# Second group's first layer interleaved with the end of the first group's second layer, and VectorE's order fixed by hand in that stage

## The chip, the cores and the metric

The kernel runs on one core of one Trainium2 chip. The metric is the device time in microseconds of one execution. A core has TensorE (matmuls; the profile calls it PE, and its weight loads PEld), VectorE (DVE), ScalarE (ACT), GpSimd (POOL) and SyncE (SP). Each of them works through its own list of instructions in order, and they wait for one another by semaphores. SyncE here only issues DMAs, and GpSimd issues those that fetch the weights.

## What is computed

```python
# q, k, v, a_re, a_im: (B=4, H=8, S=768, D=48)
mag = sqrt(a_re**2 + a_im**2)
a = (a_re + 1j * a_im) * minimum(mag, 0.999) / (mag + 1e-6)
for t in range(S):                       # a recurrence over complex states
    S_ = a[t][:, None] * S_ + outer(k[t], v[t])
    y[t] = q[t] @ S_.real
x = y as (B*S = 3072, H*D = 384)         # rows are tokens
h = x @ w_in                             # (3072, 2048)
out = (h * cos(h)) @ w_out               # (3072, 384)
```

The first part is an attention with gated, complex decay; the second is a two-layer block. The layer weights arrive as 64-bit floats, which the kernel turns into 32-bit floats itself.

## The kernel before, in words

**Tiling.** The 3072 tokens are cut into chunks of 128 steps, and two chunks make a group; there are twelve groups (`NG`). Within a chunk the recurrence is done with matmuls: the decays are turned to logarithms and angles, summed along the chunk by a matmul with a triangular matrix, and give factors for keys and queries.

**What a group does.** In order of the data:

- `g_log` takes logarithms of the decays on ScalarE and VectorE. `p_powers` sums them on TensorE (tile `lgs`) and takes exponentials. `g_angle` is an arctangent, `p_even` (three VectorE operations, which also store the last row to DRAM and read it back as `end`), `g_carry` (a carry from the chunk before, and a split in an upper half `hi` by ScalarE and a lower half `lo` by VectorE), `g_phase` (summed angles on TensorE, tile `phs`, a cast on ScalarE, a subtraction on VectorE).
- `p_apply`, `g_trig` and `g_stack` make the stacked keys `ks` and queries `qs`. From group 2 on `f_transpose` transposes them in blocks on VectorE (tile `tr`), and a round trip through DRAM (`moved`) gives `kT` and `qT`. Of these DMAs qT's comes last.
- For each chunk `f_scores` makes the scores on TensorE (tile `sc`) and masks them on VectorE (`atm`), `f_state` carries the state (`sp`), `f_out` makes the chunk's output (`yp`), which ScalarE copies to `yT`. `f_xt` stores yT to DRAM (`x`) and reads it back as `xT`, the input of the first layer.
- First layer: `mm1_sums` makes six matmuls into one tile `hp` (128 x 512), for two of the sixteen blocks of h; I call this a pair. `mm1_gate` follows: ScalarE takes the sine of it (with half pi added) and a square sum (`junk`), and VectorE multiplies (`gate`). A group has eight pairs.
- Second layer: `mm2` multiplies four (or `nj`) blocks of gates with w_out into the tile `op`, for one chunk. Only groups 0 and 1 do it in this plain form; later ones (`seventh`) use seven products of half size.

**PSUM.** There are eight banks of 128 x 512 floats: the pool `pa` has five (tag "a": lgs, phs, sc, sp, yp), and `pm` has three (tags "m", two, and "acc", one: hp, op, sum).

**Weights.** GpSimd's queue fetches w_in and w_out in 64-bit parts (`raw`), and `as_floats` converts each part: two VectorE operations, one on ScalarE, and a last one on VectorE. `convert(back[4:])` are the last four of w_out's eight parts, each two of the sixteen blocks j.

**Order.** TensorE's list is a chain in the order in which the program emits its matmuls, ScalarE's table functions are another, and `weave` spreads several lists of steps over a stage by fractions. For VectorE and the rest of ScalarE and SyncE a scheduler picks the order, except while `Ordered.by_hand` is true, when VectorE's and ScalarE's operations are chained as emitted; that holds for the start of group 0. The stage that changes is this one: group 0's second layer, the preparation of group 2, and group 1's first layer, one after another on TensorE. After it a loop over n from 2 on weaves the attention of group n, the second layer of n − 1, the preparation of n + 1 and the first layer of n. Inputs of a group beyond it (`load`) go through SyncE's queue, which also carries the DMAs of `f_xt`, `p_even`, `f_transpose` and the stores of the output.

Of the kernel before, what the change touches and what calls it, by code (L numbers as in the profile page):

```python
# [11 lines left out]
F32 = mybir.dt.float32  # L12
# [475 lines left out]
def fast_path(ctx, tc, q, k, v, a_re, a_im, moe_w_in, moe_w_out, out, least, odd, wide):  # L488
# [8 lines left out]
    DM, DF = moe_w_in.shape  # L497
    C = 128
    NCH = S // C
    G = 2  # L500
# [20 lines left out]
    pa = ctx.enter_context(tc.tile_pool(name="pa", bufs=5, space=PSUM))  # L521
# [22 lines left out]
    Y = [dict() for _ in range(N)]  # L544
# [104 lines left out]
    tail = {}  # L649
# [15 lines left out]
    class Ordered:  # L665


        by_hand, mark = False, {}

        def __init__(self, engine, name):  # L670
            self.engine, self.name = engine, name
# [1 line left out]
        def __getattr__(self, op):  # L673
            def call(**kw):
                ins = getattr(self.engine, op)(**kw)  # L675
                if Ordered.by_hand:
                    chain(ins, self.name)
                elif self.name in Ordered.mark:
                    behind(ins, Ordered.mark[self.name])
                return ins  # L680
            return call
# [120 lines left out]
    def p_even(g, i, n):  # L802


        x = X[g]
        u = cut(x["mag"], i, n)
        P, Q = cut(x["P"], i, n), cut(x["Q"], i, n)
        ins = [vector.scalar_tensor_tensor(out=u, in0=Q, scalar=HUGE, in1=P,
                                           op0=ALU.min, op1=ALU.mult)]
        for t in P, Q:  # L810
            ins.append(vector.scalar_tensor_tensor(out=t, in0=u, scalar=3.0, in1=t,
                                                   op0=ALU.subtract, op1=ALU.mult))

        for one_, what in zip(ins, ("carried", "split")):
            if what in x:
                behind(one_, x[what])
        row = x["row"][ds(i * DM, n * DM)]
        nc.sync.dma_start(out=row, in_=P[C - 1:C].rearrange("o x -> (o x)"))
        end = x["end"][:, ds(i * H, n * H)]
        for a in range(2):  # L820
            nc.sync.dma_start(out=end[ds(a * D, D)], in_=row.rearrange("(x d) -> d x", d=D))
# [8 lines left out]
    def p_apply(g, i, n):  # L830
        x = X[g]
        P, Q, u = (cut(x[name], i, n) for name in ("P", "Q", "mag"))
        vector.tensor_tensor(out=Q, in0=cut(x["k"], i, n), in1=Q, op=ALU.mult)
        vector.tensor_tensor(out=u, in0=cut(x["q"], i, n), in1=P, op=ALU.mult)

    def g_angle(g, i, n):

        at = cut(X[g]["tan"], i, n)
        special(out=at, in_=at, func=AF.Arctan)
# [4 lines left out]
    def g_carry(g):  # L844

        n, some = g * G, ds(C - 32, 32)
        if g >= PEG and n % NCH:
            head = cut(X[g]["tan"], 0, 1)[some]
            X[g]["carried"] = vector.scalar_tensor_tensor(
                out=head, in0=before(n)[some], scalar=carry[some], in1=head,  # L850
                op0=ALU.mult, op1=ALU.add)
        if g >= PEG:
            X[g]["split"] = upper_half(g, cut(X[g]["tan"], 0, G), 1.0 / math.pi)()
# [161 lines left out]
    def mm1_sums(g, jp):  # L1015
        x = X[g]
        x.setdefault("gate", {})
        order = x.setdefault("order", [])
        home = "mmc"[len(order) % 3]
        order.append(jp)  # L1020
        pool, tag, bufs = {"m": (pm, "m", 2), "c": (pm, "acc", 1)}[home]
        ps = pool.tile([C, 2, G * C], F32, tag=tag, name="hp", bufs=bufs)
        for ji in range(2):
            for dc in range(ND):
                matmul(ps[:, ji], lhsT=w_in[:, jp, dc, ts(ji, C)],
                       rhs=x["xT"][:, dc].rearrange("p g t -> p (g t)"),
                       start=(dc == 0), stop=(dc == ND - 1))
        x.setdefault("hp", {})[jp] = ps
# [16 lines left out]

    def mm2(g, i, j0, nj):
        if j0 == 0:
            Y[g * G + i]["op"] = pm.tile([C, DM], F32, tag="acc" if i == 0 else "m", name="op",
                                         bufs=1 if i == 0 else 2)
        ps = Y[g * G + i]["op"]  # L1050
        for j in range(j0, j0 + nj):
            matmul(ps, lhsT=X[g]["gate"][j // 2][:, j % 2, ts(i, C)], rhs=w_out[:, j],
                   start=(j == 0), stop=(j == NJ - 1))
        if j0 + nj == NJ:
            ot = msb.tile([C, DM], F32, tag="ot", name="ot")
            scalar.mul(out=ot, in_=ps, mul=1.0 / (in_scale * out_scale))
            nc.sync.dma_start(out=out[ts(g * G + i, C), :], in_=ot)
# [85 lines left out]
    def products(g, lo, hi):  # L1143
        if g < PLAIN:
            return []
        return [lambda p=p, part=part: seventh(g, p, part)
                for p in range(lo, hi) for part in range(2)]
# [4 lines left out]
    def weave(*parts):  # L1152

        items = []
        for p, (part, lo, hi) in enumerate(parts):
            part = list(part)
            items += [(lo + (hi - lo) * (i + 0.5) / len(part), p, t)
                      for i, t in enumerate(part)]
        for _, _, t in sorted(items, key=lambda x: x[:2]):
            t()  # L1160

    def each(step, g):
        return [lambda i=i, n=n: step(g, i, n) for i, n in spans(g)] if 0 <= g < NG else []

    def keys(g):

        if not 0 <= g < NG:
            return
        for i, n in spans(g):
            yield lambda i=i, n=n: g_trig(g, i, n)  # L1170
            yield lambda i=i, n=n: (g_stack(g, i, n), p_end(g, i, n))
            for name in "kT", "qT":
                if g >= PEG:
                    yield lambda i=i, n=n, name=name: f_transpose(g, i, n, name)
# [4 lines left out]
    def powers(g):  # L1179
        return [lambda i=i: p_powers(g, i) for i in range(G)]  # L1180

    def prods(g):
        if not 0 <= g < NG:
            return
        if g not in (1, 2):
            yield from powers(g)
            yield lambda: g_angle(g, 0, G)
        yield lambda: g_carry(g)
        yield lambda: (p_even(g, 0, G), p_apply(g, 0, G))

    def logs(g):
        yield from each(g_log, g)
        if 0 <= g and g + 1 < NG:
            yield lambda: load(g + 1, ("re", "im"))

    def phases(g):
        return [lambda i=i: g_phase(g, i) for i in range(G)] if 0 <= g < NG else []
# [11 lines left out]
    def first(g):  # L1209
        order = range(NJ // 2) if g < PLAIN else (0, 4, 1, 5, 2, 6, 3, 7)  # L1210
        return [lambda jp=jp: mm1(g, jp) for jp in order]

    def second(g, i):
        return [lambda j0=j0: mm2(g, i, j0, 4) for j0 in range(0, NJ, 4)] if g < PLAIN else []

    def convert(parts):
        return [lambda dst=dst, src=src: weight(dst, src)() for dst, src in parts]
# [22 lines left out]
    chain(nc.gpsimd.tensor_copy(out=alls, in_=one_b.to_broadcast([C, C])), "gpsimd")  # L1240
    early = [weight(dst, src) for dst, src in into[:RAW]]
    chain(nc.gpsimd.tensor_copy(out=exact, in_=ones), "gpsimd")
    Ordered.by_hand = True
    preload("natural_log_exp_and_others")
    busy(27)
    one, two = (log_steps(0, i, 1) for i in range(2))
# [16 lines left out]
    g_stack(0, 0, 1)  # L1263
    p_apply(0, 1, 1)
    g_stack(0, 1, 1)
    Ordered.by_hand, Ordered.mark = False, dict(tail)
    steps = log_steps(1, 0, G)
    log = [lambda: next(steps, None)]
    for t in (turned(0, 0, "kT") + turned(0, 0, "qT") + early[:1]
# [8 lines left out]
    def sums(g, lo, hi):  # L1278
        return [lambda jp=jp: mm1_sums(g, jp) for jp in range(lo, hi)]

    def gates(g, lo, hi):
        return [lambda jp=jp: mm1_gate(g, jp) for jp in range(lo, hi)]

    later = convert(into[RAW:])
    for t in (sums(0, 0, 2) + [lambda: g_angle(1, 0, G)] + later[:1] + phases(1)[:1]
# [5 lines left out]
          (keys(1), 0.3, 0.8), (convert(back[:1]), 0.9, 1.0))  # L1291
    over = [t for i in range(G) for name in ("kT", "qT") for t in turned(1, i, name)]
    weave((over, 0.0, 0.2), (chunks(1), 0.2, 1.0), (convert(back[1:4]), 0.1, 1.0),
          (logs(2), 0.7, 0.71))
    both = [t for pair in zip(second(0, 0), second(0, 1)) for t in pair]
    weave((both, 0.0, 0.5), (convert(back[4:]), 0.0, 0.3), (powers(2), 0.3, 0.34),
          ([lambda: g_angle(2, 0, G)], 0.35, 0.36), (prods(2), 0.36, 0.4),
          (phases(2), 0.47, 0.53), (keys(2), 0.53, 0.6), (first(1), 0.5, 1.0))
    room.close()
    stage.update(pool=ctx.enter_context(tc.tile_pool(name="late", bufs=1)), bufs=1)  # L1300
    for n in range(2, NG):
        weave((mixes(n - 1, 2, 4), 0.0, 0.12), (logs(n + 1), 0.0, 0.02), (chunks(n), 0.0, 0.36),
              (second(n - 1, 0), -0.08, 0.28), (products(n - 1, 0, 3), 0.0, 0.36),
              (prods(n + 1), 0.25, 0.27), (second(n - 1, 1), 0.4, 0.56),
              (products(n - 1, 3, 7), 0.4, 0.56), (phases(n + 1), 0.44, 0.54),
              (keys(n + 1), 0.53, 0.66), (quarters() if n == PLAIN else [], 0.4, 0.9),
              (last_quarter() if n == PLAIN else [], 0.9, 1.0), (first(n), 0.56, 1.0),
              (mixes(n, 0, 2), 0.9, 1.0), (guarded(n - 1, per) if n > 3 else [], 0.1, 0.9))
# [77 lines left out]
```

## Time and profile before

| | |
|---|---|
| median of 3 runs | 670.77 us (670.17 to 672.28) |
| profiled execution | 672.38 us; its span 670.6 us |
| TensorE's granted clock over the span | 0.993 |

By stretches of the span, busy us of each engine, from the profile:

| stretch, us | what | PE | DVE | ACT | clock |
|---|---|---|---|---|---|
| 0 to 60 | start, group 0's attention, part of its first layer | 52.0 | 46.1 | 47.0 | 0.97 |
| 60 to 96.5 | rest of it, group 1's attention, first half of group 0's second layer | 34.8 | 35.4 | 29.6 | 1.00 |
| 96.5 to 137 | the stage that changes | 35.8 | 27.4 | 17.2 | 0.96 |
| 137 to 168 | group 2's attention, group 1's second layer | 31.0 | 26.2 | 19.5 | 1.00 |
| 168 to 240 | groups 2 and 3 | 71.1 | 55.5 | 40.0 | 1.00 |
| 240 to 670.6 | groups 4 to 11 | 422.2 | 299.6 | 239.7 | 1.00 |

How to read the lines that follow: a time is in microseconds from the span's start. L686 is the helper that emits every matmul, L675 the one that emits VectorE's and ScalarE's ordered operations and L706 the table functions, so that groups are told apart by their tiles ("hp<-xT,w_in" writes hp and reads xT and w_in). A matmul of 32-bit floats shows as two records. In a line of waits stand the engine and tile that waited, the one waited for, then the total, how many times, and the longest. In a line of short windows stand the window, its length, the busy time (and records) of PE, PEld, DVE, ACT and POOL, the granted clock, the busy share of the DMA engines and GB/s.

### The profile page before, as it was taken

To read this page: it belongs to the slowest core of one execution; us is meant where nothing else is said; L and a number is where in the kernel's file an instruction comes from. 1 tells how busy PE (TensorE), PEld (TensorE's weight loads), DVE (VectorE), ACT (ScalarE), POOL (GpSimd) and SP (SyncE) were. 2 spreads that over 40 slices of the span, in tenths; PEclk is the share of its full clock that TensorE was granted. 3 is DMA by queue.
4 is the path that set the end of the run, shared out by engine and by line. 5 is a ranking of instruction groups with operands and counts; after the bars stand their busy time and mean duration, and the time that the engine had idled before them with its cause. 6 is when DMAs were issued, how large, how long until landed. Compare 5 with 4: busy or idle time off the path is not lost.

```text
span 670.6 us, 10717 instructions
## 1 busy us (share of the span) xinstructions
PE 646.9 (96%) x4053; PEld 576.6 (86%) x4053; DVE 490.2 (73%) x793; ACT 392.9 (59%) x728; POOL 28.6 (4%) x47
## 2 busy tenths in 40 slices
PE   7899989899999999999999999999999999999996
PEld 5687857676899889899899989999999999999895
DVE  4999997578877877877868878778778778862251
ACT  6886866374474475576476476467467467332330
POOL 2011100000000000000000000000000000000000
PEclk8999999899999999999999999999999999999999
DMA  9967665715915746845946845865865853363000
GB/s 249 199 188 195 205 178 108 184 29 105 218 45 110 198 112 133 225 107 129 237 107 131 223 118 119 218 137 119 218 136 119 217 137 92 112 140 106 25 6 24
DMA packets 232810, 94.90 MB, mean 142 GB/s; under 512 B 208798, under 2 KB 221217, under 8 KB 232748
## 3 DMA queue, kind: packets, MB, share of 16 engines
q1 hardware_dynamic: 226252, 68.62, 45.3%
q0 software_dynamic: 5632, 25.17, 11.5%
q8 instruction: 34, 0.56, 0.3%
q10 hardware_dynamic: 864, 0.33, 0.2%
q14 instruction: 28, 0.23, 0.1%
HBM read 69.28 MB, written 24.81 MB: 140 GB/s over the span
## 4 chain that ended last, share of the span: by engine, by line
PE 78%; DMA 8%; DVE 7%; ACT 4%; issue 1%; SPq 0%; ACTq 0%; DVEq 0%
PE hp L686 33%; PE op L686 15%; PE sum L686 13%; PE sc L686 5%; PE yp L686 5%; PE sp L686 3%; DMA qT<-moved 2%; DMA raw<-in_moe_w_out_dram 2%; PE phs L686 2%; DMA re<-in_a_re_dram 1%; DVE mag L675 1%; DVE tan L675 1%; PE lgs L686 1%; DMA im<-in_a_im_dram 1%; DMA raw<-in_moe_w_in_dram 1%
## 5 line engine op out<-in xcount | busy, mean ns | idle before, releaser
L686 PE MATMUL hp<-xT,w_in 128*128 128x256 f32 x1152 | 253.5, 381 | 4.7 <-DVE gate L675 2.9
L686 PEld LDWEIGHTS hp<-xT,w_in 128*128 128x128 f32 x1152 | 219.4, 191 | 36.7 <-DVE gate L675 3.3
L706 ACT ACTIVATE gate<-hp,half_pi_b 128x512 f32<-128x512 f32 x96 | 65.9, 686 | 129.9 <-PE hp L686 129.9
L675 DVE TENSOR_TENSOR gate<-hp,gate 128x512 f32<-128x512 f32 x96 | 65.6, 684 | 58.5 <-ACT junk L675 58.5
L686 PE MATMUL op<-w_out,gate 128*128 128x192 f32 (+1 forms) x448 | 102.6, 375 | 1.8 <-DVE w_out L675 1.8
L686 PEld LDWEIGHTS op<-w_out,gate 128*128 128x128 f32 x448 | 75.8, 190 | 19.4 <-DVE w_out L675 3.0
L675 ACT ACTIVATE junk<-hp 128x512 bf16<-128x512 f32 x96 | 56.5, 589 | 0.0
L686 PE MATMUL sum<-t_s,s 128*128 128x192 f32 x320 | 55.3, 326 | 0.0
L686 PEld LDWEIGHTS sum<-t_s,s 128*128 128x128 f32 x320 | 52.5, 190 | 0.1
L686 PE MATMUL sc<-qT,kT 96*128 96x128 f32 x384 | 49.1, 276 | 2.2 <-DMA qT<-moved 1.3
L686 PEld LDWEIGHTS sc<-qT,kT 96*128 96x128 f32 x384 | 47.4, 192 | 4.4 <-DMA qT<-moved 1.3
L675 DVE TENSOR_TENSOR atm<-sc,causal 128x512 f32<-128x512 f32 x48 | 32.9, 687 | 24.0 <-PE sc L686 23.8
L675 ACT ACTIVATE ot<-sum 128x192 f32<-128x192 f32 x30 | 9.5, 319 | 49.4 <-PE sum L686 49.4
L675 DVE SCALAR_TENSOR_TENSOR ot<-op,ot 128x192 f32<-128x192 f32 x31 | 10.9, 353 | 32.5 <-ACT ot L675 24.0
L686 PE MATMUL yp<-atm,v 128*48 128x128 f32 x352 | 33.5, 277 | 0.0
L702 ACT ACT_TABLE_LOAD x24 | 30.8, 1283 | 4.0 <-DMA ident<-ident_const 3.6
L686 PEld LDWEIGHTS sp<-v,ks 128*96 128x96 f32 x320 | 29.8, 165 | 0.3 <-issue 0.2
L686 PE MATMUL sp<-v,ks 128*96 128x48 f32 x320 | 29.6, 245 | 0.0
L686 PE MATMUL yp<-qT,state 96*48 96x128 f32 x304 | 29.6, 272 | 0.0
L686 PE MATMUL sum<-w_out,gate 128*128 128x192 f32 x160 | 29.6, 329 | 0.0
L686 PE MATMUL op<-t_a,gate 128*128 128x192 f32 x160 | 29.0, 332 | 0.0
L675 ACT CAST tan<-phs 128x384 int32<-128x384 f32 x24 | 11.5, 478 | 28.8 <-PE phs L686 28.8
(138 smaller groups left out, 991.4 us busy)
## 6 DMA issues: line engine op xcount, KB each, us to landing
moved<-tr SPq DMA_DIRECT2D x20, 768.0 KB
raw<-in_moe_w_in_dram POOLq DMA_DIRECT2D x16, 768.0 KB, 5.6
raw<-in_moe_w_out_dram POOLq DMA_DIRECT2D x16, 768.0 KB, 4.9
kT<-moved SPq DMA_DIRECT2D x40, 192.0 KB
qT<-moved SPq DMA_DIRECT2D x10, 768.0 KB
k<-in_k_dram SPq DMA_DIRECT2D x24, 192.0 KB
q<-in_q_dram SPq DMA_DIRECT2D x24, 192.0 KB
v<-in_v_dram SPq DMA_DIRECT2D x24, 192.0 KB
```

The lines of the kernel that those rows point to most:

```text
L675: ins = getattr(self.engine, op)(**kw)
L686: chain(nc.tensor.matmul(out, **kw), "tensor")
L702: chain(nc.scalar.preload_act_table_set(table))
L706: chain(nc.scalar.activation(func=func, **kw))
```

## The change

The stage's two weaves of steps become an order written out by hand. Two pairs of group 1's first layer come ahead of the third quarter of group 0's second layer, four more after it, then two quarters of group 1's own second layer (`upper[:2]`), the last quarter of group 0's, and the last two pairs. For this, `hp` of group 1 moves to the pool `pa` (home "a"), and the two `op` tiles swap tags for group 1. The last two conversions of w_out move behind gates 3 and 4. From `sums(1, 0, 1)` on, VectorE's operations are chained in the order in which they are written, ScalarE's are not (`by_hand` becomes a tuple of names). The load of group 3's re and im moves from before the stage into it. In the loop at n = 2 the remaining two quarters (`upper[2:]`) replace the four of `second(1, 0)`, and `second(n - 1, 1)` moves from 0.40 to 0.56 to 0.36 to 0.50.

```diff
@@ class Ordered
-        by_hand, mark = False, {}
+        by_hand, mark = (), {}
...
-                if Ordered.by_hand:
+                if self.name in Ordered.by_hand:
@@ mm1_sums
-        home = "mmc"[len(order) % 3]
+        home = "mmc"[len(order) % 3] if g != 1 else "a"
         order.append(jp)
-        pool, tag, bufs = {"m": (pm, "m", 2), "c": (pm, "acc", 1)}[home]
+        pool, tag, bufs = {"m": (pm, "m", 2), "c": (pm, "acc", 1), "a": (pa, "a", 5)}[home]
@@ mm2
-            Y[g * G + i]["op"] = pm.tile([C, DM], F32, tag="acc" if i == 0 else "m", name="op",
-                                         bufs=1 if i == 0 else 2)
+            Y[g * G + i]["op"] = pm.tile([C, DM], F32, tag="acc" if g == i else "m", name="op",
+                                         bufs=1 if g == i else 2)
@@ the order of the stages
-    Ordered.by_hand = True
+    Ordered.by_hand = "vector", "scalar"
...
-    Ordered.by_hand, Ordered.mark = False, dict(tail)
+    Ordered.by_hand, Ordered.mark = (), dict(tail)
...
-          (logs(2), 0.7, 0.71))
-    both = [t for pair in zip(second(0, 0), second(0, 1)) for t in pair]
-    weave((both, 0.0, 0.5), (convert(back[4:]), 0.0, 0.3), (powers(2), 0.3, 0.34),
-          ([lambda: g_angle(2, 0, G)], 0.35, 0.36), (prods(2), 0.36, 0.4),
-          (phases(2), 0.47, 0.53), (keys(2), 0.53, 0.6), (first(1), 0.5, 1.0))
+          (each(g_log, 2), 0.7, 0.71))
+    def pair(j0, nj):
+        return [lambda i=i: mm2(0, i, j0, nj) for i in range(G)]
+
+    upper, there, turning = second(1, 0), convert(back[4:]), list(keys(2))
+    for t in pair(0, 4) + there[:1] + pair(4, 4) + powers(2) + [lambda: g_angle(2, 0, G)]:
+        t()
+    Ordered.by_hand = "vector",
+    for t in (sums(1, 0, 1) + there[1:2]
+              + [lambda: p_even(2, 0, G), lambda: g_carry(2)] + sums(1, 1, 2)
+              + pair(8, 2)[:1] + gates(1, 0, 2) + phases(2) + pair(8, 2)[1:] + pair(10, 2)
+              + [lambda: load(3, ("re", "im"))]
+              + turning[:1] + [lambda: p_apply(2, 0, G)] + turning[1:2]
+              + sums(1, 2, 4) + turning[2:3] + gates(1, 2, 3) + turning[3:] + gates(1, 3, 4)
+              + sums(1, 4, 6) + there[2:3] + gates(1, 4, 5) + there[3:] + gates(1, 5, 6)
+              + upper[:2] + pair(12, 4) + first(1)[6:]):
+        t()
+    Ordered.by_hand = ()
     room.close()
...
-              (second(n - 1, 0), -0.08, 0.28), (products(n - 1, 0, 3), 0.0, 0.36),
-              (prods(n + 1), 0.25, 0.27), (second(n - 1, 1), 0.4, 0.56),
+              (upper[2:] if n == 2 else [], 0.0, 0.2), (products(n - 1, 0, 3), 0.0, 0.36),
+              (prods(n + 1), 0.25, 0.27), (second(n - 1, 1), 0.36, 0.5),
```

## The prediction

> **What bounds the kernel now.** I read the page's busy shares first, then whom TensorE waited for, then the chain of waits around the change, the granted clock in short windows, and last SyncE's DMA queue. The busy shares and the chain's summary:
>
> ```profile
> PE 646.9 (96%) x4053; PEld 576.6 (86%) x4053; DVE 490.2 (73%) x793; ACT 392.9 (59%) x728; POOL 28.6 (4%) x47
> ...
> PE 78%; DMA 8%; DVE 7%; ACT 4%; issue 1%; SPq 0%; ACTq 0%; DVEq 0%
> ```
>
> TensorE is busy 96% of the span and is most of the chain. Matmuls have to be done either way, so an edit of the order can win only TensorE's gaps and its slow stretches, or make new ones. In the waits, the largest and the third largest of TensorE's gaps belong to the stage that changes:
>
> ```profile
> PE hp L686 <- DVE gate L675: 2.9, 1, 2.9
> PE lgs L686 <- DVE lg L675: 2.6, 2, 2.1
> PE op L686 <- DVE w_out L675: 1.8, 2, 1.5
> ```
>
> The chain in order of time shows where they lie (start, length, what):
>
> ```profile
> 95.89 0.87 DVE w_out L675
> ...
> 97.63 2.22 DVE w_out L675 x3
> ...
> 99.89 1.56 PE op L686 x4
> 101.45 0.69 PE lgs L686 x4
> 102.14 7.74 PE op L686 x24
> 109.88 1.04 PE phs L686 x6
> 110.93 10.37 PE hp L686 x48
> ...
> 121.36 2.19 DVE tr L675
> 123.55 0.59 DVE gate L675
> ...
> 124.18 12.31 PE hp L686 x48
> ```
>
> At 96.5 the second layer has caught up with VectorE's conversion of w_out: TensorE waits 0.30 us and then 1.52 us, 1.82 together. From 121.3 to 124.18 the first layer of group 1 waits 2.89 us for a gate product, which stands behind two transposes on VectorE while all three banks of `pm` hold sums. Then two equal halves (48 records, 24 matmuls each) take 10.37 and 12.31 us. The granted clock says why the second is 1.94 us longer (the figure before the DMA share):
>
> ```profile
> 124.00:125.00 1.00, 0.82 (x4) 0.75 (x5) 1.00 (x3) 0.00 (x0) 0.00 (x0) 1.00 0.75 307
> 125.00:126.00 1.00, 1.00 (x5) 0.86 (x4) 0.32 (x1) 0.00 (x0) 0.00 (x0) 0.72 0.95 332
> 126.00:127.00 1.00, 1.00 (x4) 0.73 (x4) 0.00 (x0) 0.00 (x0) 0.00 (x0) 0.50 0.98 240
> 127.00:128.00 1.00, 1.00 (x4) 0.82 (x3) 0.00 (x0) 0.00 (x0) 0.00 (x0) 0.50 1.26 198
> 128.00:129.00 1.00, 1.00 (x5) 0.80 (x4) 0.00 (x0) 0.50 (x1) 0.00 (x0) 0.57 1.29 202
> ```
>
> After the 2.89 us gap the clock falls to a half; after the 1.52 us gap at 98.4 it stayed at 1.00. So the stage loses 1.82 + 2.89 + 1.94 = **6.65 us**, all on TensorE.
>
> **What the Trainium skill says.** (1) "TensorE: Matmul & The Clock Gate", Part 1: an idle TensorE drops to half clock after about one idle window of 3.4 us and wins it back by about as much steady work. The trace agrees in kind: half clock from 125.3 to 128.9, after 2.9 us idle. (2) "DMA: Bandwidth & Descriptors", Anatomy of one DMA: a transfer has some 2 us of fixed cost, mostly the confirmation of its last byte. Here xT is issued at 163.98 and its first matmul starts at 167.96, 3.98 us, an upper bound for 384 KB and its confirmation. (3) "PSUM — Partial Sum Buffer", Specifications: eight banks of 2 KB a partition; the kernel divides them 5 (`pa`) and 3 (`pm`), and one `hp` tile fills one. No further page bears on it.
>
> **The change, part by part.** No instruction is added or removed; the built program has new orders on TensorE, VectorE, ScalarE and SyncE, and up to 92 us all of them are as before. GpSimd's queue does not change. I follow the new orders with the old durations. A 128x768 VectorE operation follows the last after 0.87 us, or 1.0 if it needs its result; a first-layer pair (`mm1_sums`, six matmuls) takes 10.37/4 = 2.59; an op matmul 7.74/12 = 0.645.
>
> *Gaps removed.* TensorE's new order: 16 op matmuls (both chunks, j 0 to 7, done at 96.51 as now), lgs, two pairs of the first layer, 2 op, phs, 6 op, four pairs, 16 op, two pairs, then scores of group 2. The third conversion's end, 98.9 + 0.5 = 99.4 here, is wanted only at about 106, so 1.82 goes. `hp` now takes `pa`'s five banks. The rotation makes pair 7 the first to want a bank of pairs 2 to 7, that of pair 2: its gate product ends at 115.7 (below), pair 7 starts at about 133. So 2.89 goes, and with no gap that long the slow clock's 1.94 goes as well.
>
> *New wait at phs.* TensorE: 96.51 + lgs 0.69 = 97.20; two pairs 5.19, 102.39; 2 op, 103.68. The phase needs the other chain. ScalarE: exponentials 0.38 after lgs starts (101.45 to 101.83 now), 96.89, four in 1.65, table load 1.28, arctangent 0.84: 100.68. VectorE: conversion until 99.4, then by the written order mag, lg, Q and carry, which ends at 102.8 (0.62 for the carry). ScalarE's `hi` takes 0.84 to 103.65, VectorE's `lo` 0.95 to 104.65. The second phs matmul wants lo: a wait of **0.9 us**. Behind it on TensorE stand 6 op and all else. From below 0.3 (if `hp` starts later, it hides), above 1.8: the last raw transfer (ScalarE waits for it till 95.52 now) shares the engines with xT, which moved up, and ScalarE has the exponentials behind it.
>
> *xT.* `f_xt`'s last DMA now stands ahead of four re DMAs and all of im, and can be issued at 92.6 to 93.2; with 3.98 it is there at 96.6 to 97.2. TensorE wants it at 97.20 instead of 110.9. I take 0, from 0 to 1.
>
> *VectorE's fixed order.* Phase subtractions until 107.0 (cast 0.48 each on ScalarE), cosine ready at 108.7, four products to 112.75, tr of ks 115.1, gate 2 115.7, tr of qs 117.95, gate 3 118.6, conversion 121.0, gate 4 121.6, conversion 124.0. TensorE: phs done 105.6, 6 op 109.5, four pairs 119.9, 8 op of group 1 (they need gates 0 to 3, last 118.6) 125.0, 8 op that need the two last conversions (121.0, 124.0) 130.2, two pairs **135.4**. No wait; the cover is 2 us or more. The late transposes cost nothing for the same reason: qs ends 5.6 us earlier than now (123.55), so qT lands before 135.4, as it does before 139.07 now.
>
> *After the stage.* Now 4 matmuls of group 1's chunk 0 (2.58) are done before scores start at 139.07; then 8 will be, at 135.4. So stage for stage TensorE is 139.07 − 135.4 + 2.58 = 6.2 us ahead, which is 6.65 less the 0.9, rounding aside. But these matmuls no longer cover what follows. Counted from the last `hp` end (T), TensorE does half the scores (0.9), op 2.58, the other half 0.9, sp 1.32, yp 1.9, op 2.58: the second chunk's scores start at T + 10.3 with the hand-overs, lgs at T + 12.1, yp at T + 12.8. VectorE's order puts mag, lo and tan of group 3 ahead of the chunk's masks, and ScalarE's chain (last `hp` to lo's end is 136.49 to 148.32 now, 11.8) allows lo no sooner: then tan until T + 12.6, mask 13.25 (0.65), tan again 14.1, mask 14.75. yp needs the masks at T + 12.8 and T + 13.75: about **1.0 us** of new waits (0.3 to 1.6). Now 4 op matmuls (2.58) stand between scores and yp and hide this. Later, phs's second half comes right before the first layer of group 2; the op matmuls behind it (2.58) moved ahead. Qs, its transposes and qT's round trip hang on that phs. Now it ends at 165.38, and qT is there by 187.0 (the DMA engines fall idle after 186), 21.6 later; scores want it at 188.6. Then they want it 20.8 after phs's end: **0.7 us** (0 to 2, by how full the DMA engines are).
>
> *xT of group 2*: asked for at T + 27, there at T + 26 to 26.8; 0. *Loads of re, im, k*: they leave SyncE 1 to 3 us later, 25 us ahead of use. *Stores of out* move behind qT; nobody waits for them.
>
> Sum: 6.65 − 0.9 − 1.0 − 0.7 = 4.05, and I take 4.1. The profiled execution took 672.38 (span 670.6), 1.6 above the median of 670.77; it becomes 668.3, and the median **666.7**.
>
> **The rivals.** *Full gain (0.14).* Masks are ordered late only on paper and the phase meets a late `hp`: 6.65 less at most 1.0, so 664.6. For it: the two losses after the stage rest on margins of 1 us. Against: VectorE runs in order.
>
> *Given back (0.22).* All three new waits are at their upper end, 1.8 + 1.6 + 2.0 = 5.4: gain 1.3, 669.5; half of this case lies within 2 us. For it: qT waits (0.9 at 239.94) show that the round trip has no slack. Against: k, q and v of the next group are issued further ahead of it.
>
> *Slower (0.10): xT is late.* The first layer starts 13.7 us sooner, and if xT's data wait behind raw and re, TensorE stands at 97.2 with nothing else in its order. If it were issued where it is now (100.62), it came at 104.5: a gap of 7.3, which brings back the slow clock (1.94) and hides the phs wait: −6.65 + 1.94 + 7.3 + 1.0 + 0.7 = +4.3, 675.1. It decides from an arrival after 102.2, where the sum is +2. Against: its place in SyncE's order.
>
> *The change doesn't do what it says (0.02)*: the scheduler keeps the gaps; 670.8. The built order speaks against it.
>
> **How the numbers follow.** The likeliest case (0.52) spans gains of 2.5 to 5.7. About 0.3%, 2.0 us, is what a measurement of this kernel tells from no change. Faster: 0.52 + 0.14 + 0.11 = 0.77; same: 0.11 + 0.02 = 0.13; slower: 0.10. The range goes from 663.7 (6.65 off with no new wait at all, and 0.4 more if the wait for group 2's xT, 0.4 now, goes too) to 670.5 (the third case with xT 1 us late at the start as well). It leaves out the slower case, no effect, and the tails.
>
> **What would show it.** Right: no TensorE wait for gate near 121 and none for w_out; clock 1.00 from 97 to 136; phs waiting about 0.9 near 104; scores of group 2 near 135.4; waits of yp for atm near 149 and of sc for qT near 183. Wrong: a wait of `hp` for xT near 97; a clock below 1; scores later than 138, which would mean that VectorE's fixed order is late for gates or w_out.

## The result, and the profile after

| kernel | median, us | ratio to before, 95% interval | its profiled execution: time, span | clock |
|---|---|---|---|---|
| before | 671.43 (20 runs) | 1 | 672.38, 670.6 | 0.993 |
| after | 668.52 (20 runs) | 0.9954 (0.9941 to 0.9967) | 668.10, 666.3 | 0.995 |

The change makes the kernel faster by 0.46% (0.33 to 0.59), which is 3.1 us (2.2 to 4.0) of 671.4. The prediction had taken 4.1 off, just outside this interval: from the 670.77 of three runs to 666.7, which from the 671.43 of twenty would be 667.3. A second set of 7 runs of the same kernel gave 668.22 and 0.9962 (0.9942 to 0.9982).

Busy shares and the chain's summary, of after:

```profile
PE 646.1 (97%) x4053; PEld 576.2 (86%) x4053; DVE 490.6 (74%) x793; ACT 393.3 (59%) x728; POOL 28.0 (4%) x47
...
PE 76%; DMA 6%; DVE 4%; ACT 3%; issue 1%; SPq 0%; DVEq 0%; ACTq 0%
```

Every engine has as many instructions as before (4053 records on TensorE, 646 us). What changed is idle time and, in the stage, the clock. TensorE's waits, of after:

```profile
PE sc L686 <- DMA qT<-moved: 0.6, 1, 0.6
...
PE sc L686 <- issue: 0.7, 1, 0.7
...
PE hp L686 <- DVE gate L675: 0.8, 1, 0.8
...
PE hp L686 <- DMA xT<-x: 0.5, 1, 0.5
PE yp L686 <- issue: 0.5, 1, 0.5
```

The gate wait of 2.9 and the waits for w_out are gone. New are five short ones: for xT, two at yp (0.5 here, 0.3 in the timeline below), a gate wait of 0.8 and one at sc of 0.7 that the profile puts down to "issue", that is to nothing it could name; the record of semaphores shows below that it is qT. (The line with qT<-moved is another stage.) The chain in order of time shows the stage itself without a gap once xT is there:

```profile
91.61 0.65 SPq L564
92.36 5.30 DMA xT<-x
97.67 0.14 issue
97.80 5.42 PE hp L686 x24
103.22 1.29 PE op L686 x4
104.51 1.19 PE phs L686 x6
105.70 3.87 PE op L686 x12
109.57 10.36 PE hp L686 x48
119.93 10.32 PE op L686 x32
130.25 5.19 PE hp L686 x24
```

xT is issued at 92.36, slightly before the 92.6 to 93.2 that were predicted, and lands 5.30 us later. Its first matmul starts at 97.80, 5.44 us after the issue and not 3.98, and 0.6 later than TensorE could have started. From there to 135.4 TensorE works without a pause, in equal steps (5.42 for two pairs, 10.36 for four, 5.19 for two). The clock, of after, in windows over the stage (1.00 before the DMA share in each):

```profile
97.00:104.00 7.00, 6.53 (x29) 5.24 (x29) 5.99 (x8) 6.25 (x12) 0.00 (x0) 1.00 0.30 51
104.00:121.00 17.00, 17.00 (x72) 13.33 (x71) 15.01 (x20) 8.12 (x18) 0.00 (x0) 1.00 0.48 117
121.00:125.00 4.00, 4.00 (x14) 2.35 (x13) 3.90 (x6) 0.23 (x2) 0.00 (x0) 1.00 1.12 255
125.00:130.00 5.00, 5.00 (x17) 2.97 (x16) 1.40 (x2) 0.49 (x1) 0.00 (x0) 1.00 1.03 216
```

Where the rest went shows in TensorE's timeline of after, from the scores of group 2 to those of group 3 (start, length, engine, line, operation, tiles, records; in brackets the idle time ahead of it and what ended it):

```profile
135.26 1.06 PE L686 MATMUL sc<-qT,kT 96*128 96x128 f32 x8
...
148.74 0.43 PE L686 MATMUL yp<-atm,v 128*48 128x128 f32 x4 [0.46 <-issue]
...
150.16 0.43 PE L686 MATMUL yp<-atm,v 128*48 128x128 f32 x4 [0.33 <-DVE atm L675]
...
162.65 7.93 PE L686 MATMUL hp<-xT,w_in 128*128 128x256 f32 x36
171.33 13.35 PE L686 MATMUL hp<-xT,w_in 128*128 128x256 f32 x60 [0.75 <-DVE gate L675]
185.39 1.13 PE L686 MATMUL sc<-qT,kT 96*128 96x128 f32 x8 [0.71 <-issue]
```

The same view of before, whose waits at yp, gate and sc are missing because there are none:

```profile
138.91 1.95 PE L686 MATMUL sc<-qT,kT 96*128 96x128 f32 x16
...
167.80 20.94 PE L686 MATMUL hp<-xT,w_in 128*128 128x256 f32 x96
188.57 1.06 PE L686 MATMUL sc<-qT,kT 96*128 96x128 f32 x8
```

At its first scores after has already done 2.58 us of second layer that before still has ahead of it. With these, TensorE is 138.91 − 135.26 + 2.58 = 6.2 us ahead at the scores of group 2, 167.80 − 162.65 = 5.2 at the first layer of group 2, and 188.57 − 185.39 = 3.2 at the scores of group 3. It arrived with 6.2 and lost 1.0 at yp and 2.0 in the first layer of group 2. In later groups the distance in these two traces lies between 3.0 and 4.4 us, and their spans differ by 4.3; the medians differ by 2.9.

### The profile page after: what moved, and what is told of

Same layout as the page of the kernel before. It is cut to its first block, busy times and chain, and to the rows that moved or that the text cites. A ratio compares the mean times of both kernels' runs of the same rounds, so it can differ in the third digit from the quotient of the medians.

```text
span 666.3 us, 10717 instructions
## 1 busy us (share of the span) xinstructions
PE 646.1 (97%) x4053; PEld 576.2 (86%) x4053; DVE 490.6 (74%) x793; ACT 393.3 (59%) x728; POOL 28.0 (4%) x47
## 4 chain that ended last, share of the span: by engine, by line
PE 76%; DMA 6%; DVE 4%; ACT 3%; issue 1%; SPq 0%; DVEq 0%; ACTq 0%
PE hp L686 32%; PE sum L686 15%; PE op L686 14%; PE yp L686 5%; PE sc L686 5%; PE sp L686 3%; DMA raw<-in_moe_w_out_dram 2%; DMA xT<-x 1%; PE phs L686 1%; DMA qT<-moved 1%; PE lgs L686 1%; DVE mag L675 1%; DMA q<-in_q_dram 1%; ACT rs L706 1%; DVE atm L675 0%
```

## The experiments

Theory: the gaps and the slow clock are won in the stage as worked out, and what follows hands about half back, because each part that starts earlier meets the next transfer or mask that can't. Rivals: the loss is the two new margins that the change itself made (op matmuls moved away from behind phs and from behind the scores), so that putting them back gives it back; or the gain comes from one part (the banks, VectorE's order) and the rest does nothing.

To compare the profiles apart from how the start went, I also give the time from the start of group 1's last scores, which no edit reaches (80.73 in before), to the first scores of group 3: 107.84 us in before, 104.55 in after, 103.97 in its second set.

| kernel | that time, against before | median, us | ratio (95%) |
|---|---|---|---|
| after | −3.3 | 668.52 | 0.9954 (0.9941 to 0.9967) |
| after, second set | −3.9 | 668.22 | 0.9962 (0.9942 to 0.9982) |
| op behind phs again | −4.9 | 667.56 | 0.9947 (0.9929 to 0.9964) |
| op behind the scores again | −5.1 | 667.65 | 0.9950 (0.9933 to 0.9967) |
| both of these | −4.8 | 667.60 | 0.9941 (0.9923 to 0.9960) |
| before with the banks alone | −3.0 | 669.53 | 0.9973 (0.9961 to 0.9985) |
| after without the fixed order of VectorE | −1.3 | 671.30 | 1.0001 (0.9987 to 1.0015) |
| after with re and im ahead of xT | +4.8 | 678.03 | 1.0090 (1.0064 to 1.0116) |
| before with matmuls in the gap | −0.7 | 670.34 | 0.9987 (0.9974 to 1.0000) |

The profile of one execution and the medians differ by up to 1.4 us here; the execution of before that was profiled was itself some 1 us above its median. A part of that spread can come from the start: near 14 us the traces have a stretch of half clock that lasts 3.4 us in some (before, after) and 6.8 us in others (without the fixed order, with the gap filled), which is up to 1.7 us.

**The second layer back behind phs.** After, with the second half of the second layer where before has it:

```diff
-              (prods(n + 1), 0.25, 0.27), (second(n - 1, 1), 0.36, 0.5),
+              (prods(n + 1), 0.25, 0.27), (second(n - 1, 1), 0.4, 0.56),
```

> The changed kernel with one part undone: the second layer of group 1's second chunk is back at 0.40 to 0.56 in the loop, so four op matmuls (2.58 us) stand between the second half of phs and the first layer of group 2 again. Theory (what the change loses after its stage is the round trip of qT, which hangs on phs and lost the 2.58 us that covered it): phs ends about 2.6 us earlier for the same start of hp, the wait of the scores for qT near 185 (0.71) and the wait of hp for gate 0 near 171 (0.75) go, and the first layer of group 2 takes 20.8 us as before, not 22.7. The gain over before grows from 3.1 to about 5.0 us: 0.9926. Rival (the 2 us are lost to other things, such as DMA traffic that the earlier stage pushed into this one): the scores still wait for qT, and the ratio stays at 0.9954.

Measured 0.9947 (0.9929 to 0.9964). Its timeline of TensorE:

```profile
104.30 0.45 PE L686 MATMUL phs<-lo,exact 128*128 128x384 f32 x1 [0.56 <-DVE lo L675]
...
162.41 20.88 PE L686 MATMUL hp<-xT,w_in 128*128 128x256 f32 x96
183.47 1.13 PE L686 MATMUL sc<-qT,kT 96*128 96x128 f32 x8 [0.17 <-issue]
```

The first layer of group 2 runs in one piece of 20.88, and of the two gaps of after (0.75 in it and 0.71 behind it) 0.17 is left: the first layer with the hand-over takes 21.1 us instead of 22.7. So both gaps hang on the 2.58 us of op matmuls that the change took from between phs and this layer. The sharper end of this expectation was missed in the total: the ratio's interval overlaps that of after, so the better time is seen in the trace and not shown by the medians. xT came in time here (first layer at 96.87), and then phs did wait 0.56 for lo, as the prediction had worked out (0.9).

**The second layer back behind the scores.** After, with the two remaining quarters of group 1 later:

```diff
-              (upper[2:] if n == 2 else [], 0.0, 0.2), (products(n - 1, 0, 3), 0.0, 0.36),
+              (upper[2:] if n == 2 else [], 0.07, 0.27), (products(n - 1, 0, 3), 0.0, 0.36),
```

> The changed kernel with the last two quarters of group 1's chunk 0 (upper[2:]) at 0.07 to 0.27 of the loop instead of 0 to 0.2: one quarter then stands between sp and yp of the first chunk, one between the scores of the second chunk and lgs. Theory (the waits of yp for the masks near 149, 0.8 us together, come from the second layer's quarters having moved ahead, so that nothing stands between scores and yp): these waits go, the first layer of group 2 starts 0.8 us earlier; phs moves with it, so that the scores wait for qT as long as in the changed kernel. Ratio 0.9942. Rival (the masks are late because VectorE is full there): TensorE waits as long, at yp or at lgs; 0.9954.

Measured 0.9950 (0.9933 to 0.9967). From its timeline:

```profile
161.67 21.19 PE L686 MATMUL hp<-xT,w_in 128*128 128x256 f32 x96 [0.72 <-DMA xT<-x]
183.00 1.13 PE L686 MATMUL sc<-qT,kT 96*128 96x128 f32 x8
```

No yp line has a wait any more, so op matmuls between scores and yp are what covers the masks. But 0.72 comes back as a wait for group 2's xT, which after did not have. That wait stands between phs and the first layer, as the op matmuls did, and the gaps for gate and qT disappear with it.

**Both.**

> The changed kernel with both edits: the quarters of the second chunk back at 0.40 to 0.56, so that one stands behind phs, and upper[2:] at 0.07 to 0.27. Theory: of the changed kernel's three later losses the waits of yp (0.8) and of gate and qT in group 2's first layer (1.9 together) go; what stays are xT and phs at the stage's start (0.6 together). Gain 3.1 + 0.8 + 1.7 = 5.6 us over before, 0.9917; at least the 0.9947 of the run with the one edit. Rival (the losses after the stage move on to the next wait, such as xT of group 2, of which there was 0.4 before): half of that, 0.9938.

Measured 0.9941 (0.9923 to 0.9960), the rival's case: with phs and yp covered, nearly the whole of what is lost after the stage (1.6 us) is one wait.

```profile
163.27 20.99 PE L686 MATMUL hp<-xT,w_in 128*128 128x256 f32 x96 [1.31 <-DMA xT<-x]
```

The three versions have the same median within 0.1 us. None is shown to be faster than after by these intervals, though each is ahead of it in the trace. What is left is a loss that moves from mask to gate to transfer.

**The banks alone.** Before, with `hp` of group 1 in the five banks and nothing else:

```diff
-        home = "mmc"[len(order) % 3]
+        home = "mmc"[len(order) % 3] if g != 1 else "a"
...
-        pool, tag, bufs = {"m": (pm, "m", 2), "c": (pm, "acc", 1)}[home]
+        pool, tag, bufs = {"m": (pm, "m", 2), "c": (pm, "acc", 1), "a": (pa, "a", 5)}[home]
```

> The kernel before with one part alone: hp of group 1 in the five banks of pa. TensorE's order is that of before. Theory (three banks make the 2.89 us gap, the gap makes the slow clock): no wait for gate near 121, clock 1.00 from 125 to 129, so 4.83 us earlier at the first scores of group 2; the two waits for w_out (1.8) stay. These scores then come at about 134.2, and qT, whose transposes are not moved, is there at about 135.4 (11.85 us after the transposes' end, as near 185 in the changed kernel): a wait of about 1.2. Gain 3.6 us, 0.9946, as much as the whole change. Rival (the interleaving is what does it, the banks are a detail): a wait for gate of 2 us or more stays and the ratio is above 0.998.

Measured 0.9973 (0.9961 to 0.9985), 1.8 us. Its timeline:

```profile
100.19 1.56 PE L686 MATMUL op<-w_out,gate 128*128 128x384 f32 x4 [1.52 <-DVE w_out L675]
111.07 20.88 PE L686 MATMUL hp<-xT,w_in 128*128 128x256 f32 x96
136.53 2.02 PE L686 MATMUL sc<-qT,kT 96*128 96x128 f32 x16 [2.00 <-DMA qT<-moved]
...
165.49 20.88 PE L686 MATMUL hp<-xT,w_in 128*128 128x256 f32 x96
```

The first layer is now 20.88 in one piece, so the banks alone remove the gap and the slow clock, 4.8 us. Then the scores of group 2 wait 2.00 for qT, whose transposes on VectorE have not moved: more than I had expected. After that nothing is lost: the matmuls behind the scores and behind phs are still there, and group 2's first layer has no gap. So at the scores of group 3 the banks alone are 3.0 us ahead of before, where the whole change is 3.3 ahead in its first trace and 3.9 in its second. The medians put it 1.3 us behind the whole change by the ratios, but the two intervals overlap. That the order by hand adds more to the banks than the 0.3 to 0.9 us of the traces is therefore not shown, and the rival that one part brings most of the gain is not excluded. The new order with `hp` left in the three banks was not run.

**VectorE's order left to the scheduler.** After without `Ordered.by_hand = "vector",` in the stage:

> The changed kernel with VectorE's order in the stage left to the scheduler; TensorE's order is the same. In its order a conversion step stands between mag and lg, both gate products stand before lo, ScalarE's hi comes after the second gate, and the third of the last conversions comes ahead of the transposes. Theory (the order by hand keeps phs from waiting): lo comes about 2.2 us later, after gate 1 (sine, square sum and product), TensorE waits about 2.2 us for phs near 104 where it waits 0.15 now; transposes end some 3 us later with qT still in time for the scores (10 us of cover now). 2 us slower than the changed kernel, 1.0 us faster than before, 0.9985. Rival (VectorE has cover everywhere and its order is worth nothing): 0.9954.

Measured 1.0001 (0.9987 to 1.0015): the whole gain is gone, more than expected. Its timeline of TensorE:

```profile
105.70 0.45 PE L686 MATMUL phs<-hi,exact 128*128 128x384 f32 x1 [0.80 <-ACT hi L675]
106.69 0.45 PE L686 MATMUL phs<-lo,exact 128*128 128x384 f32 x1 [0.55 <-DVE lo L675]
```

Between 96 and 103.5 VectorE has five operations on w_out ahead of mag, lg and Q or among them (three in after), and ends the carry's add at 104.3 (102.6 in after); ScalarE takes the gate of the second pair ahead of hi. phs then waits 1.35 us, where after had none to speak of, and with the restarts TensorE is 1.7 us longer from the op matmuls ahead of phs to those behind it. xT costs 0.2 less, and at the end the way from group 2's first layer to the scores, where qT is waited for 1.11 (0.71), is 0.4 longer. That makes the 2.0 by which the trace is behind after. That the transposes would end later was wrong (119.5, 119.7 in after). The medians show some 3. The mean granted clock of its 22 runs is 0.9934, that of the 20 of after 0.9947, and 0.0013 of 670 us is 0.9 us: the last microsecond may be there, but in which stage is not shown.

**xT behind re and im.** After with the loads of re and im issued where before has them, ahead of xT:

```diff
-          (each(g_log, 2), 0.7, 0.71))
+          (logs(2), 0.7, 0.71))
...
-              + [lambda: load(3, ("re", "im"))]
```

> The changed kernel with one part undone: the load of re and im of group 3 is back in front of the stage, so that xT of group 1 stands behind it on SyncE's queue (as before, where it left at 100.6). Theory (xT's place in the queue is what lets the first layer start at 97.8): xT leaves at about 100.6, hp starts at about 104.5, a gap of 7.3 us on TensorE, and the clock falls to a half for about 4 us after it (1.9 us). Against the changed kernel +6.8 + 1.9 less what phs waits (0.2) and less about 1.9 that qT waits near 185 if that has slack again: between 6.5 and 8.5 slower than it, 3.5 to 5.5 us slower than before, 1.005 to 1.008. Rival (xT would come in time from there): the ratio stays at 0.9954 within 0.001.

Measured 1.0090 (1.0064 to 1.0116), 6.0 us slower. Its timeline, and its windows of the clock:

```profile
105.98 7.72 PE L686 MATMUL hp<-xT,w_in 128*128 128x256 f32 x24 [6.59 <-DMA xT<-x]
119.75 10.52 PE L686 MATMUL hp<-xT,w_in 128*128 128x256 f32 x48
```

```profile
106.00:108.00 2.00, 2.00 (x5) 1.64 (x6) 0.56 (x1) 0.00 (x0) 0.00 (x0) 0.50 0.43 3
108.00:110.00 2.00, 2.00 (x7) 1.55 (x6) 0.00 (x0) 0.00 (x0) 0.00 (x0) 0.50 0.00 0
110.00:112.00 2.00, 2.00 (x9) 1.75 (x8) 0.00 (x0) 0.85 (x2) 0.00 (x0) 0.84 0.00 0
```

This run's stage began 2.1 us later than that of after, so 105.98 is 103.9 on its scale; the slower rival had 104.5, a gap of 7.3 (6.59 here) and 1.94 for the clock (7.72 − 5.42 = 2.3). The rival's mechanism is real, and SyncE's order is what keeps it away. The loss lies above the range that was expected: 1.0090 and not 1.005 to 1.008; against after the trace shows 8.1 us, inside the 6.5 to 8.5, and the medians 9.5.

**Matmuls in the gap.** Before, with eleven matmuls on idle tiles, which compute nothing of use, between the fourth and the fifth pair of the first layer, where TensorE has its 2.89 us gap:

```diff
-          (phases(2), 0.47, 0.53), (keys(2), 0.53, 0.6), (first(1), 0.5, 1.0))
+          (phases(2), 0.47, 0.53), (keys(2), 0.53, 0.6), (first(1), 0.5, 1.0), ([lambda: busy(11)], 0.75, 0.751))
```

> The kernel before with 11 matmuls that compute nothing of use (128x512 into a spare bank of pa, about 0.25 us each, 2.7 together) put on TensorE where it waits 2.89 us for the gate, ahead of the fifth pair of group 1's first layer; all else in the stage keeps its order. Theory (the idle gap is what takes the clock to a half): the gate comes no sooner, so the fifth pair starts near 124.2 as before, but the clock stays at 1.00 and the second half of the first layer takes 10.4 us instead of 12.3. Group 2's scores come about 1.9 us sooner, just when qT arrives (13 us after the transposes' end in the run with the banks alone, which is near 136.5): gain 1.0 to 1.9 us, 0.9971 to 0.9985. Rival (the clock falls for another reason, such as the power of what came before): the clock still falls between 125 and 129, or later, and the ratio is 1.000.

Measured 0.9987 (0.9974 to 1.0000), 0.9 us, slightly less than expected and with an interval that reaches 1; what it shows of the clock is read from the trace. Its timeline and its clock:

```profile
121.94 2.87 PE L686 MATMUL busy<-idle 128*128 128x512 f32 x11
125.22 10.63 PE L686 MATMUL hp<-xT,w_in 128*128 128x256 f32 x48 [0.41 <-DVE gate L675]
...
168.36 20.99 PE L686 MATMUL hp<-xT,w_in 128*128 128x256 f32 x96 [1.04 <-DMA xT<-x]
```

```profile
126.00:127.00 1.00, 1.00 (x6) 0.90 (x5) 0.36 (x1) 0.00 (x0) 0.00 (x0) 1.00 0.99 350
127.00:128.00 1.00, 1.00 (x7) 0.87 (x6) 0.00 (x0) 0.00 (x0) 0.00 (x0) 1.00 1.00 250
```

The wait for the gate is the same, only filled; the second half of the layer takes 10.63 instead of 12.31 and the clock stays at 1.00 where before had 0.50. So the slow stretch came from the idle time and not from the load on the chip. Of the 1.7 us won, 1.04 are lost at group 2's xT, which the expectation had not reckoned with.

**The same kernel again.**

> The changed kernel as it is, on the chip of the run with both edits, so that the two are compared with the same runs of before. Theory and rival agree: 0.9954 as measured, within 0.001.

0.9962 (0.9942 to 0.9982). Its trace repeats the picture: yp waits 0.47 and 0.33, the first layer 0.77 for the gate, sc 0.22. Only the last is smaller (0.71 in the first).

## Why the prediction was right or wrong

**Gaps removed (6.65): right, but 0.5 too small.** No w_out wait, no gate wait in the stage, clock 1.00. That the slow clock follows from the gap was argued from one trace; the filled gap shows it. The prediction calls 6.2 us (from its timeline) and 6.65 − 0.9 = 5.75 the same, "rounding aside". They are not: behind each of the two waits for w_out in before, four op records take 1.56 us, where four without a wait take 1.29 in the chains. These 0.5 us of restarting go with the waits; the timeline left them out, the sum did not count them. The 6.2 measured is what the timeline had.

**xT (0, from 0 to 1): 0.5 to 0.6.** The issue was at 92.36, slightly ahead of what was worked out; from there to the first matmul it took 5.44, against the 3.98 borrowed from group 2. Counted from group 1's last scores, the first layer starts after 16.96 us in after, 16.55 in the second set and 16.32 in the run with op behind phs, so it varies by 0.6 us.

**phs (0.9): about 0.2.** The reason that the prediction gave for its lower end held: a later `hp` hides it. With xT late by 0.5, lo ends at 104.5 just as the matmul that reads it is due; with xT in time it waits 0.56. The two together cost some 0.7 in after, where 0.9 had been taken off.

**VectorE's fixed order, no wait: right, though one step was missed.** The transposes end at 117.0 and 119.7, 1.8 to 1.9 us later than worked out, because the sine is written into the tile `lg`: ScalarE waits with it for the product that still reads that tile, which the written order puts behind the phase subtractions. Of after, ScalarE and then VectorE:

```profile
109.24 0.84 ACT L706 ACTIVATE lg<-tan 128x768 f32<-128x768 f32 x1 [3.02 <-DVE mag L675]
```

```profile
110.94 0.96 DVE L675 TENSOR_TENSOR ks<-Q,rs 128x768 f32<-128x768 f32 x1 [1.73 <-ACT rs L706]
```

The cover of 2 us and more held: scores at 135.26, predicted 135.4.

**yp (1.0): 0.8 of waits** (0.46 and 0.33), the two places named; with the refill around them TensorE lost 1.0.

**qT (0.7, from 0 to 2): 2.0, and this is the term that was mis-sized.** Two things were left out. First, the moved op matmuls also let the first layer of group 2 start 2.58 us closer to phs, and its fourth pair needs the bank of the first, whose gate product stands on VectorE behind the transpose of ks. Of after:

```profile
168.38 2.23 DVE L675 STREAM_TRANSPOSE tr<-ks 128x1536 f32<-128x1536 f32 x1
...
170.59 0.68 DVE L675 TENSOR_TENSOR gate<-hp,gate 128x512 f32<-128x512 f32 x1
```

In before the gate ended 6.1 us after the layer's start and the third pair at 7.8; in after it ends at 171.3, 8.6 after the start. That is the gate wait of 0.75, the very kind that the change removed a stage earlier, on the three banks that groups 2 and later still use. Second, I took the end of the DMA engines' work for the arrival. In quarter-microsecond windows of after (the last two figures are DMA share and GB/s):

```profile
183.75:184.00 0.25, 0.25 (x3) 0.22 (x2) 0.25 (x1) 0.00 (x0) 0.00 (x0) 1.00 0.45 115
184.00:184.25 0.25, 0.25 (x3) 0.22 (x2) 0.11 (x1) 0.00 (x0) 0.00 (x0) 1.00 0.24 66
184.25:184.50 0.25, 0.25 (x2) 0.03 (x1) 0.00 (x0) 0.00 (x0) 0.00 (x0) 1.00 0.00 0
```

The last bytes have moved by 184.4 and sc starts at 185.39, 1.0 later. The trace's record of semaphores settles what sc waited for: the transfer of qT raises its semaphore sixteen times, the last time at 185.30, 0.09 us before sc. In the second set the two stand at 184.74 and 184.83, with op behind phs at 183.37 and 183.47, without the fixed order at 187.84 and 187.94. In before the last rise is at 187.34, not 187.0, and 1.2 us ahead of sc. So from phs's end to the arrival it was 22.0 us in before and 22.5 in after, where 21.6 had been reckoned: 0.3 is the reading of before, and why after took another 0.5 is open. The Trainium skill, "DMA: Bandwidth & Descriptors", Anatomy of one DMA, which the prediction itself cites, says that the semaphore can't fire before the last byte is confirmed, and that this is most of the fixed cost; it describes transfers issued by GpSimd, and for these, issued by SyncE, the traces show 0.4 to 0.9 us from the last record to the last rise of the semaphore. The two causes don't add up: without the gate wait, sc would have waited for qT until the same 185.4. In the second set qT came sooner and only 0.22 is left behind the gate's 0.77, but there too sc starts right behind the last rise, so qT alone sets the time.

So with what was measured the sum is 6.2 − 1.0 − 2.0 = 3.2, for 4.05 forecast: 0.5 more in the stage and 1.3 less at qT. That the two errors have opposite signs is luck, and without it the forecast would have been further off. The range's lower end also counted a wait of 0.4 for group 2's xT in before; that wait is one of the weight loads (PEld), and the matmuls had none.

**The rivals.** Given back (1.3) lies below the interval, full gain (6.2 off) far above it. Slower was a sound danger: it took two lines of SyncE's order to bring it about.

## What to carry to other kernels

When a gap is closed on the engine that bounds a kernel, follow the gain until the next transfers that hang on that engine: here 6.2 us were won in the stage, and 3 us later on were lost to the masks, a gate and a round trip through memory, which were all covered before by matmuls that the change had moved. Count such filler as cover for everything behind it, not only for the wait that it visibly fills. Read a transfer's arrival at its semaphore or its consumer, not at the last moving byte. And try the smallest part of a change alone: here the freed banks without the new order were 3.0 us ahead at the scores of group 3, the whole change 3.3 to 3.9.

## What the runs showed of the hardware

The granted clock fell to a half around an idle time of 2.9 us (before), not around one of 1.5 (before) or 2.0 (banks alone); with the 2.9 us filled it did not fall. The trace's record of the clock has it at a half from 125.45 to 128.86 in before, 3.41 us, and from 103.83 to 110.65 in the run with re and im ahead of xT, 6.83 us, twice that. There TensorE had been idle from 99.4, and of the slow stretch the 4.7 us from 105.98 on cost it 2.3. The Trainium skill, "TensorE: Matmul & The Clock Gate", Part 1, gives one window of about 3.4 us for each direction, in a window that runs freely; the lengths agree with that.

But the clock also fell where TensorE was idle for only a part of such a stretch. Counted on in steps of 3.41 us from the edges in the clock's record, the stretch ahead of the fall in before runs from 122.03 to 125.45; TensorE was idle in it until 124.18, 0.63 of it. In the other run the stretch from 103.83 to 107.24, idle until 105.98, has 0.63 too and left the clock at a half. Of all stretches between 20 and 640 us in the ten traces, the idlest that kept the full clock has 0.50 (banks alone, 132.83 to 136.25). If the idle share is what counts, the limit lay between 0.50 and 0.63 here, and a gap of 2.9 us that falls evenly on two stretches would cost no clock. No run shows such a case.

A transfer's time from issue to first use varied for the same 384 KB. Issued ahead of re's and im's remaining parts, xT of group 1 reached its first matmul after 5.44 us in after and after 4.7 to 5.2 in the five other traces with that order (an upper bound where TensorE did not wait for it); issued behind them, after 3.53. From 92 to 98 the DMA engines of after were 0.94 to 1.00 busy, from 102 to 106 those of the other run 0.56 to 0.82. That the load makes the difference fits, but was not tried.
